# Output tiles of the first batch on the score banks, and instruction orders searched over 250 list schedules

## The chip, the cores and the metric

The kernel runs on one core of one Trainium2 chip. The metric is the device time of one execution in microseconds (us), lower is better. Its engines work side by side, each through a queue of its own, in order: TensorE (PE in the profile; PEld is its weight load), VectorE (DVE), ScalarE (ACT), GpSimd (POOL), and SP, which here issues nearly all DMAs. Matrix products land in PSUM, which has eight banks of 512 float32 values per partition.

## The reference

Four batches of 576 tokens. Attention of eight heads of 64 channels with a threshold: scores below the row's maximum less tau are dropped before the softmax. Then a token and channel mixer, then a gated layer with a convolution over three neighbouring tokens.

```python
scores = scale * np.matmul(q, k.transpose(0, 1, 3, 2))
thresh = np.max(scores, axis=-1, keepdims=True) - tau
attn = softmax of np.where(scores >= thresh, scores, -1e9)
x = np.matmul(attn, v), heads side by side: (4, 576, 512)
u = x + (np.maximum(x.T @ w_tok1, 0) @ w_tok2).T
u = u + np.maximum(u @ w_ch1, 0) @ w_ch2
h = np.maximum(u @ w_in, 0)
conv = sum over k of conv_w[k] * h shifted by k - 1 tokens
out = (h / (1 + np.exp(-conv))) @ w_out
```

## The kernel before, in words

**Attention of a batch** (`attention`, L701) goes through 36 iterations: four pairs of heads, nine slots of up to 128 query rows each. An iteration has the score matmuls (`scores`: L566 in batch 0, L571 in batch 1, L575 in batches 2 and 3), the negative row maximum on VectorE (L587), the exponential on ScalarE (L599), the mask, a multiply on VectorE (L606), the high half of the result as float16 on ScalarE (L611) and the low half on GpSimd (L615), a DMA transpose of both issued by SP (L620), and, five to seven iterations later, 14 matmuls with V (`pv`, L630 and L633) into bank 7. After nine slots a pair is normalised (`norm`) into xh and xl, and `tok` (L661) does the token mixer for its 128 channels: matmuls L670, L685 and L690, with an evacuation by VectorE at L693 (u_l) as the last of a tile.

**The dense part of a batch** (`dense`, L755) has four layers: L797 (w_ch1, 24 steps), L815 (w_ch2, 24 steps), L848 (w_in, 16 steps, each followed by `h_out` at L824 on ScalarE and, every second time, by the `gate`: VectorE at L833 twice and at L836, ScalarE at L831, L835 and L837, GpSimd at L838) and the output layer (`o_part`, 20 steps: L871 for the four tiles of 128 tokens, L874 for the last 64 tokens). Every product is three float16 matmuls, since weights and activations are split in a high and a low half. An output tile sums over eight gated blocks f, and `o_out` (L857) copies it out of PSUM for the store.

**Weights** arrive as 64-bit floats, 47 blocks over the first batches' time (`wload`, L355): a load (L351), then ScalarE L389, VectorE L390 and L392, GpSimd L386 or L376, then a high half (ScalarE L377) and a low half (GpSimd L378). From the ninth block on the conversion works in bank 4, which is free for other use once the last block is done.

**Banks.** Scores use pairs of banks: 0 to 5 in batch 0, 0 to 3 from batch 1 on. Dense tiles and `tok` draw theirs by `dbank()` from a list that holds 6, then 5 (once batch 1's attention begins), then 4 (once the weights are done). In the last batch, which has no attention beside it, 0 to 3 are added to the list.

**What sets the order.** The program emits batch 0's attention first, then for each batch b its dense steps, and between them a share of batch b+1's attention: after dense step i of 84, (i + 1) / (0.88 × 84) of its pieces (`FR`, L544). Over all emitted instructions `Order` (L15) then makes a list schedule. `depend` (L72) collects which instruction needs which; `run` (L154) plays the engines with a planner's costs (`cost`, `send`) and, whenever an engine is free, gives it the ready instruction that was emitted first. The order that comes out is fixed for each engine's queue, SP's included. At run time each engine follows its order and waits where something is late.

Of the kernel before, what the change touches and what calls it, by code (L numbers as in the profile page):

```python
# [2 lines left out]

# [17 lines left out]
class Order:  # L21
# [4 lines left out]
    def __init__(self, nc, tc, bank_tile, bufs):  # L26
        self.tc, self.bank_tile = tc, bank_tile
        self.group = {n: g for g, names in self.POOLS.items() for n in names}
        self.bufs = bufs
        self.ins = [i for i in nc.cur_bb.bb.instructions if len(i.outs) and self.area(i.outs[0])]  # L30
        n = len(self.ins)
        self.eng = [str(i.engine).split(".")[-1] for i in self.ins]
        self.dma = [i.opcode in ("DMACopy", "DmaTransposeAnt") for i in self.ins]
        self.before, self.first, self.uses, self.turns = [set() for _ in range(n)], [[] for _ in range(n)], [[] for _ in range(n)], {}
        self.depend()
        self.heels, turned = {}, 0
        turns = [x for x, i in enumerate(self.ins) if i.opcode == "DmaTransposeAnt"]
        for x, i in enumerate(self.ins):
            if i.opcode == "DmaTransposeAnt":
                turned += 1  # L40
            elif self.dma[x] and not self.area(i.ins[0])[9] and self.BEHIND < turned <= self.FIRST:
                heel = turned - 1 - self.BEHIND if turned <= self.LAST else self.FIRST - 1
                self.heels.setdefault(turns[heel], []).append(x)
        self.after = [[] for _ in range(n)]
        for x in range(n):
            for y in self.before[x]:
                self.after[y].append(x)
# [22 lines left out]
        return g if g in self.bufs else None  # L70

    def depend(self):  # L72
        hist, bank, wall = {}, {}, {}
        for x, i in enumerate(self.ins):
            e = self.eng[x]
            for w, a in [(0, a) for a in i.ins] + [(1, a) for a in i.outs]:
                r = self.area(a)
                if r is None or not r[9]:
                    continue
                name, q0, q1, lo, hi, step, size = r[:7]  # L80
                g = self.ring(name)
                if g:
                    if name not in hist:
                        self.first[x].append(name)
                        self.turns.setdefault(g, []).append(name)
                    if name not in self.uses[x]:
                        self.uses[x].append(name)
                if name == self.bank_tile:
                    for b in range(lo // 2048, (hi - 1) // 2048 + 1):
                        for q in range(q0, q1 + 1):  # L90
                            old, keep, others = bank.get((b, q), []), [], []
                            for y, e2, w2, l2, h2 in old:
                                over = l2 < hi and lo < h2
                                if y != x and (e2 != e or e == "PE" or over and (w or w2)):
                                    self.before[x].add(y)
                                if e2 != e:
                                    others.append(y)
                                elif e != "PE" and not (over and w and lo <= l2 and h2 <= hi) or y == x:
                                    keep.append((y, e2, w2, l2, h2))
                            bank[b, q] = keep + [(x, e, w, lo, hi)]  # L100
                            if others:
                                wall[b, q] = e, others
                            elif (b, q) in wall and wall[b, q][0] == e:
                                self.before[x].update(wall[b, q][1])
                    continue
                keep = []
                for h in hist.get(name, ()):
                    y, w2, p2, p3, l2, h2, s2, z2 = h
                    over = l2 < hi and lo < h2 and p2 <= q1 and q0 <= p3
                    if over and step and s2 == step and abs(l2 % step - lo % step) >= min(size, z2):  # L110
                        over = False
                    if over and (w or w2) and y != x:
                        self.before[x].add(y)
                        if w and lo <= l2 and h2 <= hi and q0 <= p2 and p3 <= q1 and not step:
                            continue
                    keep.append(h)
                keep.append((x, w, q0, q1, lo, hi, step, size))
                hist[name] = keep
# [29 lines left out]
        return size / 300 + 50, 500, 1450, 1750  # L148

    BEHIND, LAST, FIRST = 3, 33, 36  # L150
    LAP = {"DVE": 85, "Activation": 103, "Pool": 44}
    LAG = {"DVE": 24, "Activation": 24, "Pool": 76, "SP": 17, "PE": 30}

    def run(self):  # L154
        n = len(self.ins)
        left, ready, open_ = [len(b) for b in self.before], [0.0] * n, [False] * n
        later, now = {e: [] for e in self.LAG}, {e: [] for e in self.LAG}
# [31 lines left out]
        for _ in range(n):  # L189
            t, e = min((free[e] if now[e] else max(free[e], later[e][0][0]), e) for e in free if now[e] or later[e])  # L190
            while later[e] and later[e][0][0] <= t:
                heapq.heappush(now[e], heapq.heappop(later[e])[1])
            x = heapq.heappop(now[e])
            if self.dma[x]:
                work, issue, least, land = self.send(x)
                if len(lands) >= 8:
# [11 lines left out]
                    done = max(free[e] + least, t + 700 + work + land)  # L208
                lands.append(done)
            elif e == "PE":  # L210
                work, (rt, ct), (r0, _) = self.cost(x), self.ins[x].tile_size, self.ins[x].tile_position
                wide = self.ins[x].ins[0].dtype == F32
                if rt < 128:
                    t = max(t, rows.get(r0, 0.0), start + 4, 0.0 if tiled else end + 95)
# [6 lines left out]
                    rows, tiled, end, free[e] = {}, False, t + work, t + work  # L221
                start, done = t, t + work + 177
            else:
                work = self.cost(x)
                free[e], done = t + work - self.LAP[e], t + work + 12
            order[e].append(x)
            for z in self.first[x]:
# [13 lines left out]
            for z in self.after[x]:  # L241
# [2 lines left out]
                left[z] -= 1  # L244
                if not left[z]:
                    offer(z)
        for xs in order.values():
            for x, y in zip(xs, xs[1:]):
                self.tc.add_manual_dep(self.ins[y], self.ins[x].name, mybir.DependencyInfo(
                    mybir.DependencyClass.NoSync, mybir.DependencyReason.DATA), reason="order")  # L250


@with_exitstack
def kernel(ctx: ExitStack, tc: tile.TileContext, q, k, v, tau,
# [286 lines left out]

    LAGS = [5, 7, 7, 7]
    PER = NP * NSL
    FR = 0.88  # L544
    pair, chk, done = {}, {}, set()
    hn = S // 2

# [197 lines left out]
    late = []  # L745

    def flush():
        while late:
            bk, evac = late.pop(0)
            evac()  # L750
            free.append(bk)

    PASS = ((0, 0), (1, 0), (0, 1))

    def dense(b):  # L755
# [126 lines left out]
                tiles[j] = dbank()  # L882
                o_part(j, ps[:, tiles[j], :C if j < NS else hc], range(NG - 2))
        for j in range(NS + 1):
            bk = tiles.get(j)
            if bk is None:
                bk = dbank()
            t = ps[:, bk, :C if j < NS else hc]
            for f in range(NG - 2 if tiles else 0, NG, 2):
                o_part(j, t, (f, f + 1))  # L890
                if f < NG - 2:
                    flush()
                else:
                    late.append((bk, lambda j=j, t=t: o_out(j, t)))
                    if tiles:
                        flush()
                yield
# [16 lines left out]
    for b in range(B):  # L914
        att = attention(b + 1) if b + 1 < B else iter(())
        n = 0
        for i, _ in enumerate(dense(b)):
            while n < na * min(1.0, (i + 1) / (FR * nq)):
                next(att, None)
                n += 1  # L920
        for _ in att:
            pass
    flush()
    Order(nc, tc, ps.tensor.name, dict(x=15, st=3, wf=2, nm=6, thr=6, bias=6, rc=6, x32=1, xh=2, xl=2, rh=2, rl=2)).run()


# [56 lines left out]
```

## Time and profile before

| what | us |
|---|---|
| median of 3 runs | 766.8 |
| lowest and highest of them | 764.77, 767.48 |
| the profiled execution | 766.82 |
| its span, first to last instruction | 765.0 |
| TensorE busy | 726.6 (95% of the span) |
| VectorE, ScalarE, GpSimd busy | 508.0, 453.2, 419.1 |

The span is the time from the first to the last instruction of the profiled execution; 1.8 us of its time lie around it. A busy share is an average over stages that differ: batch 0's attention alone (to some 110 us), three stages in which a dense part runs beside the next batch's attention, and batch 3's dense part alone (from 643 us). The granted clock is that of TensorE, as a share of 2.4 GHz.

### The profile page before, as it was taken

How to read it: one execution, taken by the hardware profiler on the slowest of the kernel's cores; microseconds unless marked ns; L12 is line 12 of the kernel's file. 1: busy time of each engine (PE TensorE's matmuls, PEld its weight loads, DVE VectorE, ACT ScalarE, POOL GpSimd, SP SyncE). 2: the span in 40 equal slices, each digit the busy share in tenths (PEclk: the TensorE clock that was granted, in tenths of full speed). 3: DMA queues.
4: the chain of work that ended last, by engine and by line, in shares of the span. 5: the costliest groups of instructions: out<-in, count | busy, mean ns of one | idle time of the engine just before them, and what ended most of it. 6: DMA issues, size and time to landing. Idle time of an engine off the chain costs nothing.

```text
span 765.0 us, 18596 instructions
## 1 busy us (share of the span) xinstructions
PE 726.6 (95%) x7398; PEld 543.3 (71%) x7398; DVE 508.0 (66%) x914; ACT 453.2 (59%) x927; POOL 419.1 (55%) x463
## 2 busy tenths in 40 slices
PE   6799879999999889999999999999999999999998
PEld 3566557677776656788888756778888756788764
DVE  7988777888889962676877952676867941323470
ACT  7977767777778743665558743665557832211471
POOL 5877689798878960466555830466555730000040
PEclk9999989999999999999999999999999999999999
DMA  8999999999997602688766403678753401000001
GB/s 216 223 185 188 244 222 220 223 238 229 233 215 187 143 29 85 123 152 146 157 144 118 84 29 89 119 149 147 152 109 63 79 29 35 1 2 1 1 1 63
DMA packets 200951, 97.00 MB, mean 127 GB/s; under 512 B 174752, under 2 KB 186784, under 8 KB 200864
## 3 DMA queue, kind: packets, MB, share of 16 engines
q1 hardware_dynamic: 200544, 95.55, 59.8%
q8 instruction: 58, 0.95, 0.5%
q14 instruction: 29, 0.24, 0.1%
q10 hardware_dynamic: 320, 0.26, 0.1%
HBM read 39.35 MB, written 4.72 MB: 58 GB/s over the span
## 4 chain that ended last, share of the span: by engine, by line
PE 63%; POOL 5%; DVE 4%; ACT 4%; DMA 3%; issue 2%; SPq 0%; POOLq 0%; ACTq 0%; DVEq 0%
PE ps L815 19%; PE ps L797 12%; PE ps L871 10%; PE ps L848 6%; PE ps L575 4%; PE ps L630 3%; PE ps L670 2%; PE ps L685 2%; PE ps L633 2%; POOL ph L615 2%; PE ps L571 2%; DVE ct L833 1%; PE ps L874 1%; POOL act_t L838 1%; DMA ld<-in_v_dram 1%
## 5 line engine op out<-in xcount | busy, mean ns | idle before, releaser
L615 POOL TENSOR_TENSOR ph<-e,ph 128x576 f16<-128x576 f32 x108 | 142.5, 1320 | 106.4 <-ACT ph L611 97.0
L815 PE MATMUL ps<-act_t,wc_h 128*128 128x256 f16 (+1 forms) x768 | 150.0, 286 | 0.0
L587 DVE TENSOR_REDUCE nm<-ps 128x1 f32<-128x576 f32 x144 | 107.7, 748 | 20.6 <-PE ps L575 13.5
L606 DVE SCALAR_TENSOR_TENSOR e<-ps,thr,e 128x576 f32<-128x576 f32 x108 | 87.6, 812 | 47.8 <-ACT e L599 39.1
L838 POOL TENSOR_TENSOR act_t<-ct,act_t 128x576 f16<-128x576 f32 x32 | 46.7, 1461 | 130.8 <-ACT act_t L837 129.4
L797 PE MATMUL ps<-u_h,wc_h 128*128 128x320 f16 (+1 forms) x384 | 109.6, 286 | 1.5 <-ACT wc_h L377 0.5
L815 PE MATMUL ps<-act_t,wc_l 128*128 128x256 f16 (+1 forms) x384 | 109.7, 286 | 0.0
L797 PE MATMUL ps<-u_h,wc_l 128*128 128x320 f16 (+1 forms) x384 | 109.5, 286 | 0.0
L797 PE MATMUL ps<-u_l,wc_h 128*128 128x320 f16 (+1 forms) x384 | 109.1, 286 | 0.0
L797 PEld LDWEIGHTS <-wc_h 128*128 128x128 f16 x768 | 75.1, 98 | 22.0 <-issue 2.4
L815 PEld LDWEIGHTS <-wc_h 128*128 128x128 f16 x768 | 75.0, 98 | 20.9 <-issue 1.6
L848 PE MATMUL ps<-u_h,wi_h 128*128 128x256 f16 (+1 forms) x256 | 73.8, 288 | 5.6 <-DVE u_l L693 2.6
L871 PE MATMUL ps<-wo_h,act_t 128*128 128x512 f16 x256 | 76.4, 379 | 1.9 <-ACT h L824 1.5
L833 DVE SCALAR_TENSOR_TENSOR ct<-h,cw,ct 128x576 f32<-128x576 f32 x64 | 69.6, 1091 | 8.0 <-ACT ct L831 7.5
L772 DVE SCALAR_TENSOR_TENSOR act_t<-ps,act_t 128x256 f16<-128x256 f32 x96 | 43.6, 455 | 46.4 <-ACT act_t L771 46.3
L848 PE MATMUL ps<-u_l,wi_h 128*128 128x256 f16 (+1 forms) x256 | 73.9, 289 | 0.0
L848 PE MATMUL ps<-u_h,wi_l 128*128 128x256 f16 (+1 forms) x256 | 73.8, 289 | 0.0
L611 ACT ACTIVATE ph<-e 128x576 f16<-128x576 f32 x108 | 73.2, 678 | 1.0 <-DVE e L606 0.8
L630 PE MATMUL ps<-vh,pt 128*128 128x65 f16 (+1 forms) x1080 | 68.0, 194 | 0.1
L871 PEld LDWEIGHTS <-act_t 128*128 128x128 f16 x384 | 36.7, 98 | 43.9 <-issue 2.3
L630 PEld LDWEIGHTS <-pt 128*128 128x128 f16 (+1 forms) x1080 | 60.8, 101 | 7.4 <-issue 4.3
L771 ACT ACTIVATE act_t<-ps 128x256 f16<-128x256 f32 x96 | 38.9, 407 | 42.5 <-PE ps L797 41.6
(123 smaller groups left out, 1672.1 us busy)
## 6 DMA issues: line engine op xcount, KB each, us to landing
st<-in_moe_w_ch_dram SPq DMA_DIRECT2D x24, 512.0 KB, 4.8
ld<-in_v_dram SPq DMA_DIRECT2D x32, 160.0 KB, 3.7
kt<-ks SPq DMA_DIRECT2D x32, 144.0 KB, 2.8
st<-in_moe_w_in_dram SPq DMA_DIRECT2D x8, 512.0 KB, 4.3
st<-in_moe_w_out_dram SPq DMA_DIRECT2D x8, 512.0 KB, 5.1
out_dram<-ot SPq DMA_DIRECT2D x16, 256.0 KB, 2.0
kt<-in_k_dram SPq DMA_DIRECT2D x16, 144.0 KB, 3.7
ld<-in_q_dram SPq DMA_DIRECT2D x8, 288.0 KB, 3.4
```

Of the source, the lines that this page charges most:

```text
L587: V.tensor_reduce(out=nm, in_=c["s3"], axis=AX.XY, op=ALU.max, negate=True)
L606: V.scalar_tensor_tensor(out=e3, in0=c["s3"], scalar=c["thr"], in1=e3, op0=ALU.is_ge, op1=ALU.mult)
L611: A.activation(out=c["ph"][:, 0:S], in_=c["e"], func=AF.Copy)
L615: G.tensor_tensor(out=c["ph"][:, S:], in0=c["e"], in1=c["ph"][:, 0:S], op=ALU.subtract)
L630: T.matmul(dst[o:o + m], pt[:, j, o:o + m], vh[:, hh, j, 0:D + 1], start=(j == 0), stop=(j == NSL - 1))
L772: V.scalar_tensor_tensor(out=r_t(f, 1)[:, sl], in0=t, scalar=0.0, in1=r_t(f, 0)[:, sl], op0=ALU.max, op1=ALU.subtract)
L797: T.matmul(t, wc1[wx][:, f, c], u[c][ux][:, sl], start=(c == 0 and i == 0), stop=(c == NC - 1 and i == 2))
L815: T.matmul(t, wc2[wx][:, c, f], r_t(f, rx)[:, sl], start=(by_dve(c) and f == 0 and i == 0), stop=(f == NF - 1 and i == 2))
L833: V.scalar_tensor_tensor(out=ct, in0=ht[:, kk:kk + S], scalar=cw[:, kk, f:f + 1], in1=ct, op0=ALU.mult, op1=ALU.add)
L838: G.tensor_tensor(out=g_t(f, 1), in0=ct, in1=g_t(f, 0), op=ALU.subtract)
L848: T.matmul(t, wi[wx][:, f, c], u[c][ux][:, s0:s0 + n], start=(c == 0 and i == 0), stop=(c == NC - 1 and i == 2))
L871: T.matmul(t, g_t(f, gx)[:, j * P:(j + 1) * P], wo[wx][:, f], **lim)
```

## The change

Four of the five output tiles of batch 0 no longer draw a bank from the list: tile j takes bank j, one of the score banks 0 to 3, and does not put it on the list afterwards. The share of batch 1's attention that is emitted after dense step i of batch 0 is (i + 1) / (0.72 × 84), with 0.72 in place of 0.88, which puts its end ahead of the output layer; the other batches keep 0.88. `Order` gets a key per instruction in place of its place in the program. `search` makes the first schedule with the plain places, then 250 more: each draws one group (engine, operation, size of the output, and stretch of 1500 instructions), shifts its priority by −60, 0 or +60 places, and keeps the shift where the planner's end is not later. The order of the best is fixed as before. `depend` gets two more rules: TensorE's matmuls on one bank keep their order, and an instruction on a ring tile comes after the first of its engine on that tile.

```diff
@@ Order.__init__
+        self.costs = [None if self.dma[x] else self.cost(x) for x in range(n)]
@@ Order.depend
-        hist, bank, wall = {}, {}, {}
+        hist, bank, wall, last, opener = {}, {}, {}, {}, {}
...
+                    if opener.setdefault((name, e), x) != x:
+                        self.before[x].add(opener[name, e])
                 if name == self.bank_tile:
                     for b in range(lo // 2048, (hi - 1) // 2048 + 1):
+                        if e == "PE":
+                            if last.get(b, x) != x:
+                                self.before[x].add(last[b])
+                            last[b] = x
@@ Order
+    ROUNDS, SPAN, SHIFTS = 250, 1500, (-60, 0, 60)
+    def search(self):
+        draw, shift, kinds = random.Random(0), {}, []
+        for x, i in enumerate(self.ins):
+            kinds.append((self.eng[x], i.opcode, self.area(i.outs[0])[7], x // self.SPAN))
+        names = sorted(set(kinds))
+        key = list(range(len(kinds)))
+        best, order = self.run(key)
+        for _ in range(self.ROUNDS):
+            k = draw.choice(names)
+            old = shift.get(k, 0)
+            shift[k] = draw.choice([w for w in self.SHIFTS if w != old])
+            trial = [x + shift.get(kinds[x], 0) for x in range(len(kinds))]
+            end, got = self.run(trial)
+            if end <= best:
+                best, order = end, got
+            else:
+                shift[k] = old
+        for xs in order.values():
+            for x, y in zip(xs, xs[1:]):
+                self.tc.add_manual_dep(self.ins[y], self.ins[x].name, mybir.DependencyInfo(
+                    mybir.DependencyClass.NoSync, mybir.DependencyReason.DATA), reason="order")
-    def run(self):
+    def run(self, key):
...
-                heapq.heappush(now[e], heapq.heappop(later[e])[1])
-            x = heapq.heappop(now[e])
+                y = heapq.heappop(later[e])[1]
+                heapq.heappush(now[e], (key[y], y))
+            x = heapq.heappop(now[e])[1]
...
-        for xs in order.values():
-            for x, y in zip(xs, xs[1:]):
-                self.tc.add_manual_dep(self.ins[y], self.ins[x].name, mybir.DependencyInfo(
-                    mybir.DependencyClass.NoSync, mybir.DependencyReason.DATA), reason="order")
+        return max(free.values()), order
@@ tile_attn_mixer_kernel
-    FR = 0.88
+    FR = [0.72] + [0.88] * (B - 1)
@@ flush
             evac()
-            free.append(bk)
+            if bk is not None:
+                free.append(bk)
@@ dense, output layer
         for j in range(NS + 1):
-            bk = tiles.get(j)
-            if bk is None:
-                bk = dbank()
+            lent = b == 0 and j < NS
+            bk = j if lent else tiles[j] if tiles else dbank()
             t = ps[:, bk, :C if j < NS else hc]
             for f in range(NG - 2 if tiles else 0, NG, 2):
                 o_part(j, t, (f, f + 1))
                 if f < NG - 2:
                     flush()
                 else:
-                    late.append((bk, lambda j=j, t=t: o_out(j, t)))
+                    late.append((None if lent else bk, lambda j=j, t=t: o_out(j, t)))
@@ main loop
-            while n < na * min(1.0, (i + 1) / (FR * nq)):
+            while n < na * min(1.0, (i + 1) / (FR[b] * nq)):
...
-    Order(nc, tc, ps.tensor.name, dict(x=15, st=3, wf=2, nm=6, thr=6, bias=6, rc=6, x32=1, xh=2, xl=2, rh=2, rl=2)).run()
+    Order(nc, tc, ps.tensor.name, dict(x=15, st=3, wf=2, nm=6, thr=6, bias=6, rc=6, x32=1, xh=2, xl=2, rh=2, rl=2)).search()
```


## Rows read from the trace of the kernel before

**Rows 1.** Busy time by stage: length; PE, PEld, DVE, ACT, POOL (count); clock; DMA; GB/s.
```profile
0.00:120.00 120.00, 97.52 (x1035) 69.70 (x1036) 98.59 (x223) 88.95 (x167) 90.41 (x104) 0.94 1.02 214
120.00:225.00 105.00, 103.84 (x1107) 77.97 (x1106) 86.41 (x173) 77.20 (x151) 89.65 (x100) 1.00 1.04 229
225.00:285.00 60.00, 52.56 (x547) 36.71 (x544) 51.53 (x76) 43.07 (x84) 49.76 (x43) 0.97 0.55 122
285.00:303.00 18.00, 17.63 (x143) 10.87 (x141) 3.01 (x6) 5.13 (x11) 0.00 (x0) 1.00 0.27 88
303.00:645.00 342.00, 338.66 (x3680) 262.57 (x3679) 227.81 (x370) 201.32 (x441) 177.24 (x210) 1.00 0.55 108
645.00:765.00 120.00, 116.42 (x900) 85.46 (x897) 40.69 (x68) 37.50 (x77) 12.02 (x8) 1.00 0.03 11
sum 765.00, PE 726.65 PEld 543.28 DVE 508.03 ACT 453.16 POOL 419.08; mean PE 121.11 PEld 90.55 DVE 84.67 ACT 75.53 POOL 69.85
```

**Rows 2.** The same table for four 15-us slices with a lower granted clock.
```profile
75.00:90.00 15.00, 11.93 (x128) 8.63 (x124) 10.57 (x24) 9.74 (x17) 9.36 (x11) 0.89 1.11 223
90.00:105.00 15.00, 9.12 (x142) 6.66 (x141) 11.70 (x27) 9.43 (x20) 12.71 (x16) 0.87 0.99 224
105.00:120.00 15.00, 14.58 (x128) 10.94 (x127) 11.27 (x22) 10.47 (x21) 12.03 (x14) 0.90 1.03 244
255.00:270.00 15.00, 10.77 (x69) 7.04 (x68) 13.75 (x19) 10.36 (x21) 14.75 (x12) 0.89 0.61 111
```

**Rows 3.** TensorE timeline, 240 to 277 us; brackets: idle before, and what ended it.
```profile
243.68 0.27 PE L848 MATMUL ps<-u_h,wi_h 128*128 128x256 f16 x1 [0.89 <-ACT h L824]
...
260.49 0.30 PE L848 MATMUL ps<-u_h,wi_h 128*128 128x320 f16 x1 [2.48 <-DVE u_l L693]
...
262.17 0.47 PE L848 MATMUL ps<-u_h,wi_l 128*128 128x320 f16 x1
...
268.43 0.59 PE L871 MATMUL ps<-wo_h,act_t 128*128 128x512 f16 x2 [1.48 <-ACT h L824]
...
273.18 0.43 PE L685 MATMUL ps<-wt_h,rh 128*128 128x320 f16 x2 [1.13 <-DVE wf L392]
...
276.34 0.59 PE L871 MATMUL ps<-wo_h,act_t 128*128 128x512 f16 x2 [0.34 <-DVE u_l L693]
```

**Rows 4.** Chain that ended last, pieces of it: start us, us, what, how many.
```profile
157.08 0.69 PE ps L571 x4
...
281.25 0.12 PE ps L630 x4
...
285.21 10.38 PE ps L871 x48
```

**Rows 5.** Score matmuls of batches 2 and 3 (L575) in 225 to 285 us.
```profile
225.00:285.00 60.00, 1.47 (x8) 0.78 (x8) 0.97 0.55 122
```

**Rows 6.** VectorE and GpSimd groups in 225 to 285 us: busy us, mean ns, idle before.
```profile
L833 DVE SCALAR_TENSOR_TENSOR ct<-h,cw,ct 128x576 f32<-128x576 f32 x16 | 19.9, 1248 | 0.5 <-ACT ct L831 0.4
L587 DVE TENSOR_REDUCE nm<-ps 128x1 f32<-128x576 f32 x8 | 5.9, 740 | 0.0
L606 DVE SCALAR_TENSOR_TENSOR e<-ps,thr,e 128x576 f32<-128x576 f32 x6 | 4.8, 805 | 0.1
...
L615 POOL TENSOR_TENSOR ph<-e,ph 128x576 f16<-128x576 f32 x7 | 10.9, 1561 | 3.9 <-ACT ph L611 3.8
```

**Rows 7.** Transposes on SP in 120 to 225 us: ns issued min/median/max.
```profile
L620 SPq DMA_TRANSPOSE pt<-ph x25: 1242/1443/2445, 123.4 to 223.1; - x25
```

**Rows 8.** DMA queue of all loads, 150 to 225 us: packets, MB, share of 16 engines.
```profile
q1 hardware_dynamic: 27348, 17.36, 102.8%
```

**Rows 9.** The gates' VectorE multiply (L833) after 643 us: ns min/median/max.
```profile
L833 DVE SCALAR_TENSOR_TENSOR ct<-h,cw,ct x16: 805/816/1923, 718.5 to 743.1; 128x576 f32<-128x576 f32 x16
```

**Rows 10.** TensorE timeline, 100 to 105 us, the two longest gaps of 75 to 120.
```profile
101.94 0.24 PE L630 MATMUL ps<-vh,act_t 128*128 128x65 f16 x1 [2.39 <-DMA act_t<-act_t]
...
104.27 0.69 PE L670 MATMUL ps<-xh,wt_h 128*128 128x128 f16 x5 [1.37 <-ACT xh L658]
```

More of the change, by code (lines that the diff above doesn't have):

```diff
@@ L1 @@
 import heapq
+import random
 from contextlib import ExitStack
@@ L210, in run @@
             elif e == "PE":
-                work, (rt, ct), (r0, _) = self.cost(x), self.ins[x].tile_size, self.ins[x].tile_position
+                work, (rt, ct), (r0, _) = self.costs[x], self.ins[x].tile_size, self.ins[x].tile_position
                 wide = self.ins[x].ins[0].dtype == F32
@@ L223, in run @@
             else:
-                work = self.cost(x)
+                work = self.costs[x]
                 free[e], done = t + work - self.LAP[e], t + work + 12
```

## The prediction

> **What bounds the kernel now.** I read first the busy time of each engine by stages, with its sum [rows 1], to see which engine has no room: TensorE is busy 726.65 of 765.00 us, so 38.4 us are idle, and a new order of the same instructions can win back only such time, and time at a low clock. The profiled execution took 766.82 us, 1.8 more than its span; the median of the three runs is 766.8, so a saving on the span is taken straight off 766.8.
>
> Its rows say where the 38.4 us lie: 120 − 97.5 = 22.5 in the first 120 us (the first batch's attention, which has no dense work beside it), 1.2 in 120 to 225, 7.4 in 225 to 285 (third and output layer of batch 0 beside the last of attention 1), 0.4 and 3.4 in the next two, 3.6 in the last. In 225 to 285 VectorE is busy 51.5 of 60.
>
> Second, 15-us slices of the same table where the granted clock is not 1.00 [rows 2]: 0.89, 0.87, 0.90 and 0.89. TensorE has two levels, 1.2 and 2.4 GHz; a mean of 0.89 over 15 us is 15 × 0.11 = 1.65 us of full-speed time lost, if TensorE had work. 75 to 120 us loses at most 1.65 + 1.95 + 1.5 = 5.1, 255 to 270 loses 1.65. The last dip comes right behind the longest TensorE gap of its stretch, 2.48 us [rows 3], and a 320-column matmul goes from 0.30 to 0.47 us there.
>
> Third, TensorE's timeline in 225 to 285, for what ended each gap (in brackets at the end of a row) [rows 3]. Each ends with an instruction that gives a PSUM bank back: h_out (0.89, with a smaller one like it ahead, and 1.48), tok's u_l (2.48, 0.34), and the last weight conversion, which works in bank 4 (1.13). So here TensorE waits for banks: dense layers, tok and conversions share 4, 5 and 6, and the engines that empty them are full.
>
> **The change, part by part.**
>
> *Output tiles of batch 0 on banks 0 to 3.* Work added: none. Four of the five tiles no longer draw on 4 to 6. The three gaps from 266 us on (1.48 + 1.13 + 0.34 = 2.95) stand before output matmuls or between them: with a bank for each tile, TensorE can do (f 0 to 5) × 3 × 4 = 72 matmuls at 10.38/48 = 0.216 us [rows 4], 15.6 us of work, before the last two gates are in. I take all **2.95**; bounds 0 (the tiles then wait for the gates instead) and 2.95. The copies out on ScalarE stay five; it is busy 5.1 of 18 us in 285 to 303 [rows 1].
>
> *What is queued behind the lent banks.* Matmuls of one bank keep program order, so attention 2's first scores now wait until the tiles in banks 0 to 3 are copied out. Before, 8 such matmuls, two score tiles, ran in 225 to 285 [rows 5]. What VectorE does on two tiles, maximum and mask, is 2 × (0.74 + 0.80) = 3.1 us [rows 6] and comes behind 285. There it is busy 228 of 342 us [rows 1]. I take 0; bounds 0 and 3.1.
>
> *Pacing 0.88 to 0.72.* A dense batch has 24 + 24 + 16 + 20 = 84 steps, and the output layer begins after 64. Attention 1 was spread over 0.88 × 84 = 74 steps, now over 60.5, so it is emitted whole before the lent banks are needed. At step 48, where the third layer starts, 1 − 48/74 = 35% was still to come, now 21%. Six of its 36 masks ran in 225 to 285 [rows 6]; 6 × 21/35 = 3.6 would be left, so some 2.4 iterations move ahead of 225. They take 2.4 × 1.54 = 3.7 us of VectorE and 2.4 × 1.56 = 3.7 of GpSimd out of a stretch full on both (slice 255 to 270: 13.75 and 14.75 of 15 [rows 2]), and put 2.4 × (0.69 + 0.4) = 2.6 us of TensorE into 120 to 225, where it has no gap; 0.69 is four score matmuls, 0.4 an estimate for the 14 of attention times V from four that took 0.12 [rows 4]. Net gain 3.7 − 2.6, some **1.1**; bounds 0 and 3.7. If the 2.48 gap shrinks, the clock dip behind it may go: I take half of 1.65, **0.8**.
>
> Moved with the iterations are their transposes on SP's queue, 1.4 us of issue each [rows 7], and part of a pair's loads: some 5 us, an estimate, put into a stretch where the queue's packets already took 102.8% of the 16 engines' time [rows 8]. I cost it at 0, since TensorE had dense matmuls to do all through (1.2 us idle in 105); if that cover is gone, it costs up to 5.
>
> The gates' VectorE multiply takes 1.25 us on average in 225 to 285, 0.82 (median) after 643 us, where GpSimd does almost nothing [rows 6, 9]. The Trainium skill (SBUF — State Buffer, "Who interferes with whom") says that a VectorE instruction with two SBUF inputs contends with a GpSimd instruction that reads SBUF, and that the second fully blocks; by that the moved GpSimd work would relieve these 16 multiplies too, at most 16 × 0.43 = 6.9 us of VectorE. The sum stays by the mean as it is, since attention 1's GpSimd work is only a part of what runs beside them (the weights' low halves are as long), so I add nothing.
>
> *The search.* Same instructions, same counts; only priorities of groups move by 60 places, where the planner's own end does not get later. No trace of before prices it, so bounds: 0 below, or worse if the planner errs (a rival, below); above, what TensorE loses elsewhere. In 15 to 75 us I expect little: the queue is full there too. In 75 to 120 the idle is 3.07 + 5.88 + 0.42 = 9.4 and the clock at most 5.1 [rows 2], while VectorE has room (10.57, 11.70 of 15): the stage in which attention 0 drains and the first dense tiles are not yet ready. The two longest gaps there wait on a transpose (2.39) and on xh (1.37) [rows 10]: late by order more than by capacity. The upper bound is 14.5; I take some 30%, **4**, nearer to the lower end, since transposes there queue behind full DMA engines. The 3.4 us in 303 to 645 give **0.5**.
>
> The new dependencies (all matmuls of one bank in program order, users of a ring tile after the first one on their engine) hold in today's order as far as the trace shows it; 0.
>
> Sum: 2.95 + 1.1 + 0.8 + 4 + 0.5 = 9.35, and 766.8 − 9.35 = 757.45; I say **757.5**.
>
> **Rivals.**
>
> 1. *The search opens the lead-in.* It wins most of 75 to 120, some 12 of 14.5, and the dense stretch gives the 7.4 idle and the 1.65 of clock: 766.8 − 21 = 746. For it: the gaps are single late transfers. Against: the DMA engines are full to 120 us [rows 1], and 250 random tries over a few hundred groups are few.
>
> 2. *The planner's gain stays in the planner.* The lent banks give 2.95, the search nothing on the chip, because its durations miss what the trace shows (one multiply of 0.82 to 1.25 us); 764, no change that can be told: a measurement of this kernel tells about 0.5%, 3.8 us. That the change does not do what it says is here too: if every trial ends later in the planner, the first order stands.
>
> 3. *The DMA queue takes TensorE's place in 120 to 225.* The moved transposes and loads meet a full queue, in-order SP holds later weights behind them, and TensorE runs out of dense work: the 5 us above come due, with two dips of the clock like the one at 261 us (2 × 1.65), against 2.95 gained, so 766.8 + 5 + 3.3 − 2.95 = 772; with the 3.1 of attention 2's late start 775. I take **773**. It decides once the queue costs over 2.95 + 3.8 = 6.8. For it: 102.8%. Against: TensorE idles 1.2 of 105 us under that same queue. The Trainium skill (Perfetto Trace Analysis, "Optimization Strategy") advises interleaving regimes with different bounds; pulling attention out of the output layer undoes such a mix. The trace agrees little: in 285 to 303, output layer, VectorE is already at 3.0 of 18 us [rows 1], so there is hardly a mix left to lose.
>
> **How the numbers follow.** Forecast (751 to 763) 0.45; rival 1, 0.20; rival 2, 0.22; rival 3, 0.13. Faster 0.45 + 0.20 = 0.65, same 0.22, slower 0.13. The range leaves out rival 3 and the fast end of rival 1 (0.07): 747 to 769; that also takes in the forecast's own bounds.
>
> **What would show it.** Right: no gap over 1 us before output-layer matmuls of batch 0; granted clock 1.00 in the slice that holds its third layer; fewer than six masks of attention 1 behind the third layer's first matmul; TensorE's idle in 75 to 120 down from 9.4 to 5 or 6; TensorE's busy time about the same. Wrong: TensorE gaps in 120 to 225 that end with a transpose or a weight conversion; idle in the first 120 us at 22 or more; or a gap after the output layer of batch 0 that ends with scores waiting for a copy out.

## The result, and the profile after

The changed kernel takes 777.24 us (median of 4 runs, 776.1 to 779.87); the kernel before, on the same chip, 766.99 (4 runs). The ratio is 1.0144, with a 95% interval of 1.0111 to 1.0177: some 11 us slower, where 9 us faster had been forecast, and outside the range. The profiled execution took 776.1 us, its span is 774.2. Lines have moved by 30 or 31 (L871 is now L902, L874 is L905, L797 is L828, L630 is L660).

Busy time by stages of the kernel after, columns as in [rows 1]:

```profile
0.00:120.00 120.00, 98.05 (x1057) 70.02 (x1057) 101.02 (x228) 90.98 (x172) 92.53 (x106) 0.97 1.06 218
120.00:225.00 105.00, 100.44 (x1124) 74.79 (x1123) 86.39 (x176) 74.40 (x146) 85.17 (x95) 1.00 1.01 218
225.00:285.00 60.00, 58.55 (x547) 39.23 (x544) 46.60 (x68) 42.28 (x81) 47.75 (x44) 1.00 0.49 128
285.00:303.00 18.00, 18.00 (x108) 9.60 (x107) 2.84 (x6) 4.80 (x12) 1.03 (x2) 1.00 0.29 92
303.00:645.00 342.00, 337.12 (x3586) 257.31 (x3584) 231.05 (x369) 199.86 (x438) 175.38 (x211) 1.00 0.54 108
645.00:774.20 129.20, 125.61 (x987) 91.82 (x985) 42.14 (x70) 39.34 (x81) 11.41 (x8) 1.00 0.04 13
sum 774.20, PE 737.76 PEld 542.77 DVE 510.04 ACT 451.66 POOL 413.28; mean PE 122.96 PEld 90.46 DVE 85.01 ACT 75.28 POOL 68.88
```

Read the sum first. TensorE's idle time fell, from 38.4 to 774.20 − 737.76 = 36.4 us. Its **busy time rose by 11.1 us** (from 726.65) for the same 7398 matmuls, and that is more than the whole loss of span, 9.2 us. The weight loads (PEld) stayed: 543.3 before, 542.8 now. In 225 to 285 the idle time went from 7.4 to 1.45 and the clock from 0.97 to 1.00; in 120 to 225 idle rose from 1.2 to 4.6.

Second, the slices that answer to [rows 2]:

```profile
75.00:90.00 15.00, 9.93 (x136) 7.50 (x136) 10.63 (x22) 10.56 (x18) 10.36 (x11) 1.00 1.16 255
90.00:105.00 15.00, 10.49 (x154) 8.01 (x154) 11.51 (x27) 9.93 (x21) 13.11 (x17) 0.91 0.98 215
105.00:120.00 15.00, 14.57 (x125) 10.34 (x117) 13.25 (x26) 11.04 (x22) 12.32 (x15) 0.98 1.15 252
255.00:270.00 15.00, 13.94 (x109) 9.27 (x108) 11.65 (x19) 10.65 (x22) 14.41 (x13) 1.00 0.37 115
```

From 75 to 120 us the idle is 5.07 + 4.51 + 0.43 = 10.0, not the forecast 5 or 6. The clock there is better, though: it loses 15 × (0.00 + 0.09 + 0.02) = 1.65 us in place of 5.1.

Third, what TensorE waited for in 120 to 225 (after; total us, times, longest):

```profile
PE ps L601 <- DVE e L636: 3.0, 2, 2.1
PE ps L660 <- DVE x L683: 1.5, 1, 1.5
```

These are nearly all of the 4.6. Both end with VectorE work of attention 1, a mask and a normalisation; none ends with a transpose or a weight conversion, which rival 3 needed.

Where does busy time come from, if the matmuls are the same? TensorE's timeline in the output layer of batch 0 (after; start, duration, line, op):

```profile
273.54 0.39 PE L902 MATMUL ps<-wo_l,act_t 128*128 128x512 f16 x1
273.86 0.30 PE L905 MATMUL ps<-wo_l,act_t 128*64 128x256 f16 x1
274.09 0.39 PE L902 MATMUL ps<-wo_h,act_t 128*128 128x512 f16 x1
274.41 0.30 PE L905 MATMUL ps<-wo_l,act_t 128*64 128x256 f16 x1
274.64 0.39 PE L902 MATMUL ps<-wo_h,act_t 128*128 128x512 f16 x1
```

Read the starts, not the durations: matmuls overlap at their ends (0.39 us long, 0.216 apart). A 512-column matmul follows its like after 10.38/48 = 0.216 us [rows 4]. Here it is 0.32 to the next start, then 0.23, 0.55 a pair. The two differ in **output width**: L902 has 128 output partitions (128\*128), L905 has 64 (128\*64). The same in batch 2, where the products with V (64 wide) alternate with the first dense layer (after):

```profile
506.26 0.22 PE L660 MATMUL ps<-vh,pt 128*64 128x65 f16 x1
506.41 0.28 PE L828 MATMUL ps<-u_h,wc_l 128*128 128x256 f16 x1
506.62 0.22 PE L663 MATMUL ps<-vl,pt 128*64 128x64 f16 x1
506.77 0.28 PE L828 MATMUL ps<-u_l,wc_h 128*128 128x256 f16 x1
```

Here a 64-wide matmul of 65 columns takes 0.15 us to the next start; among its like it takes 0.03. Is it the width, or any turn from one tile and bank to another? The trace of the kernel before tells:

```profile
280.87 0.38 PE L871 MATMUL ps<-wo_h,act_t 128*128 128x512 f16 x1
281.09 0.29 PE L630 MATMUL ps<-vh,pt 128*128 128x65 f16 x4
281.21 0.38 PE L871 MATMUL ps<-wo_h,act_t 128*128 128x512 f16 x1
...
295.19 0.38 PE L871 MATMUL ps<-wo_l,act_t 128*128 128x512 f16 x1
295.50 0.41 PE L874 MATMUL ps<-wo_h,act_t 128*64 128x256 f16 x4
```

At 281 us the output layer turns to products with V in another bank and back, all 128 wide, and loses nothing: 0.22 us, then 0.12 for four. At 295 us it turns to 64-wide matmuls, and that start comes after 0.31.

The duration of a single matmul hides this. L905 and, before, L874, in groups by form (count, then busy us and mean ns):

```profile
L905 PE MATMUL ps<-wo_h,act_t 128*64 128x256 f16 x128 | 15.5, 278 | 0.0
L905 PE MATMUL ps<-wo_l,act_t 128*64 128x256 f16 x64 | 11.0, 278 | 0.0
```

```profile
L874 PE MATMUL ps<-wo_h,act_t 128*64 128x256 f16 x128 | 10.9, 274 | 0.0
L874 PE MATMUL ps<-wo_l,act_t 128*64 128x256 f16 x64 | 8.8, 272 | 0.0
```

The means, 272 to 274 and 278 ns, are 1.5 to 2% apart. (The busy time of a group counts also what runs beside it from another group. That it grew here tells that these matmuls no longer follow their like, and not what this costs.)

Counting changes between 64 and 128 wide in TensorE's order (128 rows each) gives 69 before and 184 after. By stage, each from a batch's first matmul with w_ch1 to the next batch's, in the profiled executions, "no search" being the run e2_nosearch below:

| stage, starting with | before, us | no search, us | after, us | changes before | after |
|---|---|---|---|---|---|
| the start | 111.64 | 113.02 | 108.22 | 16 | 18 |
| batch 0's w_ch1 | 188.59 | 185.18 | 191.16 | 8 | 61 |
| batch 1's | 172.27 | 173.36 | 173.16 | 20 | 20 |
| batch 2's | 170.94 | 172.63 | 179.26 | 22 | 72 |
| batch 3's, to the end | 121.56 | 121.61 | 122.40 | 3 | 13 |

The two stages that grow most against "no search", by 6.0 and 6.6 us, are the two that gained some 50 changes each.

### The profile page after: what moved, and what is told of

It is laid out like the page before. It is cut to its first block, busy times and chain, and to the rows that moved or that the text cites. A ratio compares the mean times of both kernels' runs of the same rounds, so it can differ in the third digit from the quotient of the medians.

```text
span 774.2 us, 18591 instructions
## 1 busy us (share of the span) xinstructions
PE 737.8 (95%) x7398; PEld 542.8 (70%) x7398; DVE 510.0 (66%) x914; ACT 451.7 (58%) x927; POOL 413.3 (53%) x463
## 4 chain that ended last, share of the span: by engine, by line
PE 59%; POOL 7%; DVE 7%; ACT 6%; issue 4%; DMA 3%; SPq 1%; DVEq 0%; POOLq 0%; ACTq 0%
PE ps L828 15%; PE ps L846 12%; PE ps L902 10%; PE ps L879 8%; PE ps L605 4%; PE ps L660 3%; PE ps L905 2%; POOL ph L645 2%; PE ps L715 2%; DVE ct L864 1%; PE ps L663 1%; PE ps L700 1%; DVE e L636 1%; POOL st L416 1%; ACT e L629 1%
## 5 line engine op out<-in xcount | busy, mean ns | idle before, releaser
L828 PE MATMUL ps<-u_h,wc_l 128*128 128x256 f16 (+1 forms) x384 | 109.5, 286 | 0.0
L828 PE MATMUL ps<-u_h,wc_h 128*128 128x256 f16 (+1 forms) x384 | 108.9, 286 | 0.4 <-DVE u_l L723 0.4
L828 PE MATMUL ps<-u_l,wc_h 128*128 128x256 f16 (+1 forms) x384 | 108.4, 286 | 0.0
L846 PE MATMUL ps<-act_t,wc_l 128*128 128x320 f16 (+1 forms) x384 | 106.5, 286 | 0.0
L828 PEld LDWEIGHTS <-wc_h 128*128 128x128 f16 x768 | 75.1, 98 | 22.2 <-issue 2.2
L902 PE MATMUL ps<-wo_h,act_t 128*128 128x512 f16 x256 | 78.8, 380 | 0.0
L660 PE MATMUL ps<-vh,pt 128*128 128x65 f16 (+1 forms) x1080 | 73.5, 195 | 1.9 <-DVE x L683 1.5
L803 DVE SCALAR_TENSOR_TENSOR act_t<-ps,act_t 128x256 f16<-128x256 f32 (+1 forms) x96 | 43.4, 455 | 42.6 <-ACT act_t L802 42.1
L625 POOL TENSOR_SCALAR thr<-nm,mtaus 128x1 f32<-128x1 f32 x72 | 24.6, 342 | 87.5 <-DVE nm L617 86.8
L879 PE MATMUL ps<-u_h,wi_l 128*128 128x256 f16 (+1 forms) x256 | 71.1, 286 | 0.0
L879 PE MATMUL ps<-u_l,wi_h 128*128 128x256 f16 (+1 forms) x256 | 70.9, 286 | 0.0
L660 PEld LDWEIGHTS <-pt 128*128 128x128 f16 (+1 forms) x1080 | 62.7, 101 | 9.2 <-issue 4.7
L802 ACT ACTIVATE act_t<-ps 128x256 f16<-128x256 f32 (+1 forms) x96 | 38.7, 407 | 48.6 <-PE ps L828 48.1
```

Of the source, the lines that this page charges most:

```text
L660: T.matmul(dst[o:o + m], pt[:, j, o:o + m], vh[:, hh, j, 0:D + 1], start=(j == 0), stop=(j == NSL - 1))
L803: V.scalar_tensor_tensor(out=r_t(f, 1)[:, sl], in0=t, scalar=0.0, in1=r_t(f, 0)[:, sl], op0=ALU.max, op1=ALU.subtract)
L828: T.matmul(t, wc1[wx][:, f, c], u[c][ux][:, sl], start=(c == 0 and i == 0), stop=(c == NC - 1 and i == 2))
L846: T.matmul(t, wc2[wx][:, c, f], r_t(f, rx)[:, sl], start=(by_dve(c) and f == 0 and i == 0), stop=(f == NF - 1 and i == 2))
L879: T.matmul(t, wi[wx][:, f, c], u[c][ux][:, s0:s0 + n], start=(c == 0 and i == 0), stop=(c == NC - 1 and i == 2))
L902: T.matmul(t, g_t(f, gx)[:, j * P:(j + 1) * P], wo[wx][:, f], **lim)
```

## The experiments

No kernel here leaves out any of the computation. Kernels of one group ran beside the kernel before on one chip (its medians: 764.8, 767.16, 765.73, 766.97 us), so groups are compared by their ratios. "Changes" counts changes of width in TensorE's order.

### First group: is it the search, and is it the width?

Theory A was that the search is free to alternate the widths, since the planner gives a change no price; theory B that the losses come from elsewhere in the new order.

**e1_price.** The changed kernel, with a price in the planner for each change of width:

```diff
...
-                    t = max(t, end + (95 if tiled else 0))
+                    t = max(t, end + (95 if tiled else 0 if (ct < 128) == thin else 110))
+                    thin = ct < 128
...
```

> The changed kernel with one more price in the planner: a matmul that writes 64 partitions behind one that writes 128, or the reverse, costs 110 ns more; the search, the lent banks and the pacing stay. TensorE's order then has 64 such switches, against 184 in the changed kernel and 69 before. Theory A (the search interleaves 64-wide with 128-wide matmuls, and each switch costs TensorE some 0.13 us that the planner did not know): 115 switches less are 15 us less, 777.2 - 15 = 762, in 759 to 766, and TensorE's busy time is back at some 725 us. Theory B (lent banks and pacing crowd the DMA queue in 120 to 225 us): 773 or more, TensorE busy falls little or its idle grows.

761.17 us, ratio 0.9956 [0.9943, 0.997]; 64 changes: as theory A had it. With the price in the planner, the change is a small gain. TensorE's line of the page:

```profile
PE 725.7 (95%) x7398; PEld 541.8 (71%) x7398; DVE 505.8 (66%) x914; ACT 453.4 (60%) x927; POOL 410.4 (54%) x463
```

725.7 against 737.8: the added busy time is gone.

**e2_nosearch.** The changed kernel with the first schedule only:

```diff
-    ROUNDS, SPAN, SHIFTS = 250, 1500, (-60, 0, 60)
+    ROUNDS, SPAN, SHIFTS = 0, 1500, (-60, 0, 60)
```

> The changed kernel with 0 rounds of search: lent banks, pacing 0.72 and the new dependencies alone; TensorE's order has 73 width switches. Theory A: the loss is all in the search, so this gives the lent banks' gain, 761 to 765 (766.8 less 2 to 6). Theory B: the loss is here too, 772 or more, with TensorE gaps in 120 to 225 us that end with transposes or weight conversions.

767.0, 1.0015 [0.9999, 1.0032]; 73 changes. The search alone makes the difference between 1.0015 and 1.0144, some 9.9 us. But both expectations missed: without it the change is neither a gain nor a loss, so something was also eating what the lent banks give.

**e3_search_only.** The search without the lent banks and the new pacing:

```diff
-    FR = [0.72] + [0.88] * (B - 1)
+    FR = [0.88] * B
-            lent = b == 0 and j < NS
-            bk = j if lent else tiles[j] if tiles else dbank()
+            lent = False
+            bk = tiles[j] if tiles else dbank()
```

> The search of 250 without lent banks and with pacing 0.88: banks as before. TensorE's order has 242 width switches, 173 more than before. Theory A: 766.8 + 173 x 0.13 = 789, less up to 4 that the search may win elsewhere: 783 to 791, and TensorE busy above 740 us. Theory B: no crowding without the pacing, 760 to 767.

790.83, 1.0348 [1.033, 1.0366]; 242 changes, TensorE busy 746.7 us. The search was the worst part. With the lent banks and the pacing it does less harm, and its order has 58 changes less.

**e4_alternate.** The price measured by itself, in the kernel before: in batches 1 and 2 the last full output tile and the 64-token tile are emitted in turn, one 512-column matmul, then two 64-wide ones. It makes 92 more changes and no more work.

```diff
...
+                if both:
+                    for g in (f, f + 1):
+                        for i in range(3):
+                            o_part(j, t, (g,), (i,))
+                            o_part(NS, t2, (g,), (i,))
+                else:
+                    o_part(j, t, (f, f + 1))
...
```

> The kernel before, and nothing of the change: in the output layers of batches 1 and 2 the matmuls of the fourth tile (128 tokens) and of the last 64 tokens are emitted in turn, one of 128 columns and two of 64, so that 92 width switches more stand in TensorE's order (161 against 69). Theory A: 92 x 0.11 = 10 us more, 774 to 779, all in the two output layers. If a switch costs nothing: 766 to 768.

775.71, 1.0141 [1.0127, 1.0156]. 775.71 − 764.8 = 10.9 us for 92 changes: **0.118 us each**. It lies where the changes are: the stages of batches 1 and 2 grow by 5.3 and 5.2 us for 46 changes each, their idle time stays, the others have no more changes. (TensorE's busy sum, 733.3 us, is only 6.6 above before: up to batch 1's first dense matmul the order is that of before, and yet this execution was busy 265.4 us to there, that of before 269.2. So the busy sum of one execution is good to some 4 us.) Its timeline:

```profile
462.10 0.39 PE L873 MATMUL ps<-wo_h,act_t 128*128 128x512 f16 x1
462.42 0.30 PE L876 MATMUL ps<-wo_h,act_t 128*64 128x256 f16 x2
462.65 0.39 PE L873 MATMUL ps<-wo_l,act_t 128*128 128x512 f16 x1
462.97 0.30 PE L876 MATMUL ps<-wo_l,act_t 128*64 128x256 f16 x2
```

From a 512-column start to the 64-wide pair 0.32 us, against 0.216 without a change: +0.10. Back, 0.23 for two matmuls that take 2 × 0.057 = 0.114 among their like: +0.12.

### Second group: what eats the gain of the lent banks?

**e6_deps_only.** The two new dependency rules alone: e3_search_only's edit, with 0 rounds as well.

> The kernel before with the two new dependency rules and nothing else of the change (no search, banks from the list, pacing 0.88). The rules do move rows: 452 of TensorE's 14265 listed rows differ, the first within the first batch's attention. Theory C (the rules cost the first 110 us some 1.5 us, and that is why the change without its search came out no faster): 766 to 768 where before gives 764.8, first dense matmul at 112.5 to 113 us against 111.4. If the rules cost nothing, as the prediction had it: 764 to 765.5, first dense matmul at 110.5 to 111.5.

774.31, 1.0104 [1.0086, 1.0122]: **+8.0 us** for rules that were to change nothing, more than either expectation. Sum of the stages:

```profile
sum 771.40, PE 727.02 PEld 542.72 DVE 507.24 ACT 452.40 POOL 420.68; mean PE 121.17 PEld 90.45 DVE 84.54 ACT 75.40 POOL 70.11
```

Here the busy time is that of before (726.65), and idle is up from 38.4 to 44.4: another kind of loss than the search's. SP's queue where a pair's q and k are loaded, first before:

```profile
336.70 2.85 SPq L505 DMA_DIRECT2D qt<-qs  x4
339.65 2.76 SPq L620 DMA_TRANSPOSE pt<-ph  x2
342.50 2.51 SPq L511 DMA_DIRECT2D kt<-ks  x4
```

and in e6_deps_only:

```profile
340.10 0.53 SPq L535 DMA_DIRECT2D qt<-qs  x1
341.94 1.25 SPq L650 DMA_TRANSPOSE pt<-ph  x1
343.28 1.87 SPq L535 DMA_DIRECT2D qt<-qs  x3
345.25 1.33 SPq L650 DMA_TRANSPOSE pt<-ph  x1
346.85 0.46 SPq L541 DMA_DIRECT2D kt<-ks  x1
348.62 1.24 SPq L650 DMA_TRANSPOSE pt<-ph  x1
```

Four loads into one tile stood together; now the first goes out alone, and the other three follow one transpose later. The ring-tile rule says only that they come after the first one on their queue. But the planner treats an edge as a wait until the earlier instruction is complete, for a DMA until its data has landed, and fills the planned wait with something else. (Between two matmuls, as in the bank rule, it only asks that the earlier one has started.) Orders tell which rule it is: with the bank rule alone the five orders equal those of before; with the ring-tile rule alone they are e6_deps_only's (452 of TensorE's 14265 rows differ); and with the ring-tile rule as an edge of order alone, free one tick after the start of the first, they equal those of before again.

**e5_pace_only.** e6_deps_only with the new pacing (0.72) kept.

> As the run of the rules alone, with pacing 0.72 in batch 0 as well, but the output tiles still draw banks 4 to 6. Against the run without search it lacks the lent banks alone. If the lent banks are what closed the gaps behind 240 us (6.7 us of TensorE idle before, 0.8 with pacing and lent banks), this one keeps 3 us of them or more and comes out 1 to 3 us over the run without search (767.0), 768 to 770. If the pacing closed them, it is equal to it, 766 to 768, with under 2 us idle there.

773.56, 1.0089 [1.0065, 1.0113]. Neither range holds it, as both left out the rule's 8 us. Against e6_deps_only it is −0.15%, 1.1 us, within the intervals. From here to e2_nosearch, which adds the lent banks, it is 1.0089 to 1.0015: 5.7 us are theirs.

**e8_price_nosearch.** The whole change with the price and 0 rounds.

> The whole change with the price of a width switch in the planner, but 0 rounds of search. Against the priced run with 250 rounds (761.2) it tells what the search is worth once the planner knows the price. If the search brings the gain: 766 to 768, as without price and search (767.0). If the price alone did: 760 to 763.

765.94, 0.9992 [0.9975, 1.001]. So with the price, the search takes 0.9992 to 0.9956, some 2.8 us of gain: nearly the first of the two readings.

**e7_price_nolent.** The price and 250 rounds, without lent banks and pacing.

> The search of 250 with the price of a width switch, banks from the list and pacing 0.88. Theory A says that the unpriced search without lent banks lost its 26 us by 172 width switches more; here there are 71, so it should be back at 761 to 766. If it is at 763 or more, the lent banks and the pacing are worth 2 us or more under the search (761.2 with them); if at 760 to 762, they are worth nothing.

776.36, 1.0126 [1.0107, 1.0145], a miss. The price took the search's loss away (1.0348 to 1.0126); the 8 us of the rule stayed, and the search gained nothing on e6_deps_only.

### Third group: the rule without its wait

**e14_lent_only.** Lent banks and pacing, 0 rounds, no price, the ring-tile rule as an edge of order alone:

```diff
...
-                        self.before[x].add(opener[name, e])
+                        self.behind[x].add(opener[name, e])
...
+            for z in self.chase[x]:
+                ready[z] = max(ready[z], t + 1)
...
```

> Lent banks and pacing 0.72 on today's order rules: no search, no price of a width switch, and the rule on a ring tile's first instruction kept as an order only, so that in the planner the second instruction of an engine need not wait until the first has landed. With that, the rules alone leave all five engines' orders as in the kernel before, row for row. Theory D (in the planner, that rule makes DMAs from one tile wait for each other's landing, and this cost 7 to 8 us on the chip): the run without search had 767.0 with it, so here 759 to 762, some 0.8% under before, which would be the prediction's own step for the lent banks and pacing (4.85 us) or somewhat more. If the rule is harmless beside the lent banks: 766 to 768.

**758.06, 0.9923 [0.9897, 0.9949]**; 69 changes, as before; a little faster than theory D's range. Against e2_nosearch (1.0015) the rule's wait costs 7.1 us here too. Its stages, with the sum, and what TensorE still waited for in 225 to 303:

```profile
0.00:120.00 120.00, 98.65 (x1070) 71.01 (x1070) 100.95 (x228) 91.69 (x174) 93.27 (x107) 0.96 1.00 222
120.00:225.00 105.00, 102.60 (x1139) 76.12 (x1140) 89.02 (x182) 76.63 (x148) 88.16 (x97) 1.00 1.06 228
225.00:285.00 60.00, 57.41 (x517) 38.57 (x516) 43.63 (x62) 41.17 (x79) 45.41 (x41) 1.00 0.48 107
...
sum 755.30, PE 722.20 PEld 540.85 DVE 506.16 ACT 452.97 POOL 415.68; mean PE 120.37 PEld 90.14 DVE 84.36 ACT 75.49 POOL 69.28
```

```profile
PE ps L912 <- POOL act_t L879: 1.1, 1, 1.1
PE ps L912 <- ACT act_t L878: 1.0, 2, 0.8
PE ps L889 <- DVE rl L716: 0.4, 1, 0.4
```

Idle in 225 to 285 is 2.6 against 7.4, at clock 1.00; the longest gaps that are left end with the gate (act_t), no longer with a bank being emptied [rows 3]; one of 0.4 us still does (rl, of `tok`). Batch 0's stage takes 182.0 us against 188.6, and the three behind it are those of before to 0.3 us: attention 2's late start cost nothing.

**e12_order_edge_nosearch.** e14_lent_only with the price.

> As the run before it, with the price of a width switch in the planner. TensorE's order has 67 switches against 69, so there is little for the price to save: theory D 758 to 762, within 1.5 us of the run before it. If the rule is harmless: 765 to 767, as the priced run without search (765.9).

762.65, 0.9969 [0.9953, 0.9984], a miss: a price that removes hardly a change of width (69 to 67) still moved the plan, and the time by 0.46%, clear of both intervals. In e8_price_nosearch it moved it by −0.23%, which is not clear. So an edit of the planner that hardly touches what it prices can move the time by some 3 us; what does it is not shown.

**e11_order_edge.** e12_order_edge_nosearch with 250 rounds.

> The whole change, search of 250 included, with the price of a width switch and the rule as an order only. Theory D: the search gained 4.8 us on the priced order (765.9 to 761.2); starting 6 us lower and gaining a part of that again, 753 to 759, faster than before by 1 to 1.7%. If the search merely repairs what the rule spoils, it adds nothing here: 758 to 762, as without search.

759.0, 0.992 [0.9901, 0.9938], in both ranges. Better than e12_order_edge_nosearch by 3.7 us, as the priced search gained 2.8 in the second group, and not to be told from e14_lent_only: the priced search wins back what its own first schedule had lost, and nothing that can be measured beyond the lent banks.

### Fourth group: the search, with the rule mended and no price

**e15_order_edge_unpriced.** e14_lent_only with 250 rounds.

> The whole change, with the ring-tile rule as an edge of order alone, 250 rounds of the search, and no price for a change of output width in the planner: the run with 0 rounds (0.9923 of the kernel before) plus the search. TensorE's order has 222 changes between matmuls of 64 and of 128 output partitions, against 69 without the search. Theory A (the search loses because changes of width are free in the planner): 153 more of them at 0.118 us are 18 us of TensorE, of which the search wins a few back in waits, so 768 to 776 us, ratio 1.003 to 1.013, and TensorE busy at 735 or more. Rival (the loss came from the search working around edges that waited for a completion, and goes with them): within 3 us of the run with 0 rounds, 755 to 761 us, ratio 0.986 to 0.994, TensorE busy near 722.

775.27, 1.0124 [1.009, 1.0159], as theory A had it. Sum of its stages:

```profile
sum 773.10, PE 742.54 PEld 545.03 DVE 505.63 ACT 453.77 POOL 413.88; mean PE 123.76 PEld 90.84 DVE 84.27 ACT 75.63 POOL 68.98
```

So the unpriced search loses by itself, whatever the rule. Three pairs that differ in the search alone:

| pair (no search, search) | changes | TensorE busy, us | ratio |
|---|---|---|---|
| e6_deps_only, e3_search_only | 70, 242 | 727.0, 746.7 | 1.0104, 1.0348 |
| e2_nosearch, the change | 73, 184 | 726.1, 737.8 | 1.0015, 1.0144 |
| e14_lent_only, e15_order_edge_unpriced | 69, 222 | 722.2, 742.5 | 0.9923, 1.0124 |

TensorE's busy time rises by 19.7/172 = 0.115, 11.7/111 = 0.105 and 20.3/153 = 0.133 us per added change; with sums good to some 4 us they agree with e4_alternate's 0.118.

## Why the prediction was wrong

**The sum as it came out.** The ring-tile rule in the planner +8.0 (7.1 beside the lent banks), pacing some −1, lent banks −5.7: nothing in all (1.0015). The search then adds 9.9.

**The step that failed most: "The search … 4 + 0.5".** It was costed as a gain between 0 and 14.5 us, with the planner's errors left to a rival. It cost 9.9: 111 changes of width more than e2_nosearch are 13.1 us at 0.118, and fewer waits gave some 3 of it back (idle 39.6 to 36.4). Once the planner knew this price, the search gained 2.8 and 3.7 us on its own first schedule, within the bounds of the forecast. The step took the instructions to be the same, and so TensorE's work; their neighbours were not. I wrote that no trace of before prices the search, but that trace holds 69 changes of width, and the start at 295.50 us, 0.31 behind the one before it, could have been set beside 0.216 us of [rows 4]. The planner prices a change between tiles of fewer than 128 rows and the rest (its 95), none between widths. The list schedule in program order makes few, so nothing of this showed in its times; a search that keeps whatever ends no later in the planner found them at no charge.

The Trainium skill has a sentence that the prediction should have weighed (TensorEngine Tiling (Array Packing), "Key Properties"): a change of the tiling mode drains TensorE. The traces agree in kind, as the 64-wide matmuls here are tiles of 128 × 64 to the program; the size is theirs alone.

**Second: "The new dependencies … hold in today's order as far as the trace shows it; 0".** True of the order alone, and false for the planner, which plans a wait for completion behind the ring-tile rule's edges. e6_deps_only measured +8.0, and it sits in idle time. The 4.6 us of idle in 120 to 225 are not the rule's: e6_deps_only idles 0.1 us there, and e14_lent_only, without the wait and without a search, 2.4.

**Right in sum: lent banks 2.95, pacing 1.1, clock 0.8.** Together 4.85; e14_lent_only has 765.73 × 0.0077 = 5.9, interval 3.9 to 7.9. Batch 0's stage takes 182.0 us there, 188.6 before, and 186.9 in e4_alternate, whose order is that of before up to the end of this stage. In the changed kernel no gap over 0.7 us is left in 225 to 303, and one mask of attention 1, of six, comes behind the third layer's first matmul.

That the sum holds is in part luck, as its terms do not. The lent banks alone were sized too small: 5.7 from e5_pace_only to e2_nosearch, above the bound of 2.95. The bound counted the gaps from 266 us on. With lent banks TensorE also has output work earlier: in e2_nosearch 51 output matmuls start before the third layer's last one (22 in e5_pace_only, none before), and the third layer's matmuls wait 2.4 us in 225 to 303, not 5.5.

The clock's 0.8 is not shown. The slice 255 to 270 has 1.00 after, but e4_alternate has 1.00 there too, with the order of before and 6.1 us of idle time. The dip comes and goes between executions of one order.

**Right at 0:** attention 2's late start, and the bank rule, which moves nothing in the orders of before. The full DMA queue was right at 0 in this, that no wait in 120 to 225 ends with a transfer.

**Not won: 75 to 120 us.** The idle time there was to fall from 9.4 to 5 or 6, and is 10.0. Batch 0's first dense matmul does start 3.4 us earlier (111.64 to 108.22), with less lost to the clock (5.1 − 1.65). But this start moves as much between executions of one order: up to 115 us e4_alternate and e14_lent_only have the order of before on every engine, and start at 110.70 and 108.45. So none of the 3.4 us can be put down to the search. The idle time of the first 120 us, 21.95, stands at the edge of the sign of being wrong (22). The prediction's four slices with a lower clock also leave one out, 15 to 30 us at 0.89.

**The rivals.** Rival 2 named the right place, durations that the planner gets wrong, but ended it at a gain of nothing. An optimiser with a wrong model is not neutral: it moves to where the model is wrong. Rival 3 reached the sign (773) by a mechanism that did not occur. In the list of signs, "TensorE's busy time about the same" was the line that broke, and it points straight at the cause.

**Open:** which ring tiles carry the 8 us; and why an edit that hardly touches what the planner prices moves the time by some 3 us. That e14_lent_only's TensorE is busy 4.4 us less than before need not be the change: 2.1 of it lie ahead of the first dense matmul, in the same order.

## What to carry to other kernels

A search over orders ends up in whatever its model leaves free, so price first what the present order hardly does, by an experiment like e4_alternate, and compare the searched kernel's changes of that kind with those of before. Keep "after it" and "after it is complete" apart as edges of a planner: the same rule cost 8 us as the second and nothing as the first. The lent banks with the mended rule and no search (e14_lent_only, 0.9923) beat both kernels, and no searched version measurably beat them.

## What the runs showed of the hardware

With 128 rows on both sides, a change of a matmul's output width between 128 and 64 partitions costs about 0.118 us of TensorE, some half of a 512-column matmul (0.216), and each way (+0.10 into 64, +0.12 back). A turn to another bank and line at equal width costs nothing that shows (0.22 us at 281 us). Every 64-wide matmul here is also a tile of 128 × 64, so width and tile size are not told apart. The cost does not appear as idle time, nor in a matmul's mean duration (273 to 278 ns), and hardly in the weight loads (543.3 and 542.8 us; at most 4.2 us more in a pair whose busy time grew by 20.3): only in the distance between starts and so in the busy sum.
